# VectorE's transpose of a head's P, moved behind all 16 chunks of the next head's first K piece

## The chip, the cores and the metric

The kernel runs on one core of a Trainium2 chip. The metric is the device time of one execution in microseconds (us). Three runs of the kernel before took 666.61, 669.48 and 670.76 us; their median, 669.48, is the time that the changed kernel is compared with.

## What is computed

One decode step of a transformer block, one token, in bfloat16. Attention has 32 query heads in 8 groups of 4, each group with one K/V head ("head" below means one of these 8), and a cache of 65,536 positions. A gated layer follows. Cut to what matters:

```python
# D = 512, Hq = 32, Hkv = 8, Sk = 65536, Dh = 128, F = 1792
q = layernorm(x) @ wq                                  # 32 heads of 128
scores = einsum("bhqd,bhkd->bhqk", q, k) * Dh ** -0.5  # 4 queries share a K head
p = softmax(scores, axis=-1)
o = einsum("bhqk,bhkd->bhqd", p, v)
h = x + o.reshape(1, 1, 4096) @ wo
g, u = layernorm(h) @ w_gate, layernorm(h) @ w_up
return h + (sigmoid(g) * u) @ w_down
```

K and V of one head are 16 MiB each, 256 MiB for all; the weights are small beside them.

## The kernel before

**Loads.** K and V of a head are each loaded in two pieces of 8 MiB (`PIECES`), one `dma_start` a piece, all from SyncE's queue (line 330, called from lines 338 to 342). A piece is 16 chunks of 2,048 positions. For heads h from 1 on, the loop issues K{h}.0, V{h-1}.0, K{h}.1, V{h-1}.1, in this order, and each waits until its place in the `ring` buffer is free:

- K{h}.0 waits for the marker F{h-1}.1, V{h-1}.0 for the end of the PV products of the head before it, K{h}.1 for the marker F{h}.0, V{h-1}.1 for PV{h-1}.1, the end of the first half of the PV products.
- The two K pieces overlap in the ring (`AT`: they begin at chunk 0 and chunk 4), and `ORDER` has VectorE read chunks 4 to 15 of the first piece first. So the marker F{h}.0 stands behind the 12th chunk of the piece, and F{h}.1 behind the 12th chunk of the second. A marker is a memset of one element on VectorE (line 520).

Heads are one apart: while head h's K is read and scored, V of head h-1 is multiplied with P of head h-1.

**VectorE** transposes each K chunk (line 517, 128 x 1024 as 4-byte words, from `ring` into one of 8 slots of `ktw`). From the second block on, a transpose waits until TensorE has done with the slot 8 chunks before (`S{b-1}.{c}`). It also takes the maximum of the scores (line 524), a few steps of the softmax, the transpose of P (`transposed`, lines 570 to 575: four transposes of 128 x 512 out of `P_sb` into `PT_sb`) and the sum of the denominators with its reciprocal (lines 580 and 581).

**TensorE** scores a block of 8 chunks with 32 matmuls of 512 columns (`pe_scores`). A head has four blocks, r = 0 to 3; two blocks are one K piece. Behind block r = 1 of head h it takes the denominators' matmul of head h-1 (line 578, which waits for the last transpose of P) and the first half of PV of head h-1; behind block r = 3 the second half. **ScalarE** writes P (line 563: exp of the scores, four instructions a head) at the end of a head, ahead of the next head's first block.

**Order.** Instructions are recorded by Python loops and then put out. Heads 1 to 7 are one hardware loop on VectorE and on TensorE: what is recorded under a part's name (`P.part`) becomes one section of the loop body, and `dve_flow` writes the order of VectorE's sections out by hand. `A0` to `A3` are the blocks' chunk transposes (A3 with the maxima and the softmax steps), `A4` the four transposes of P, `B0` the denominators' sum. Each engine runs its own instructions in order; engines wait for each other by semaphores.

Numbering in the text: in loop round h, "first half" means the blocks r = 0 and 1 (piece K{h}.0), "second half" the blocks r = 2 and 3 (piece K{h}.1).

Of the kernel before, what the change touches and what calls it, by code (L numbers as in the profile page):

```python
# [35 lines left out]
class Prog:  # L36
# [14 lines left out]
    def op(self, eng, fn, deps=(), name=None, to=None, times=1):  # L51
        assert name is None or name not in self.where, name
        self.ops[eng].append(dict(fn=fn, deps=[d for d in deps if d], name=name, dma=None, to=to, times=times, part=self.part.get(eng)))
        if name:
            self.where[name] = (eng, len(self.ops[eng]) - 1)
# [160 lines left out]
def bass_sequential_preLN__gqa_block_cached__glu_gated_glu__decode_kernel(  # L216
# [22 lines left out]
    with ExitStack() as es:  # L239
# [72 lines left out]
        P = Prog(nc, es)  # L312
# [187 lines left out]
        def dve_block(b):  # L500
            h, r = b // NR, b % NR
            for c in range(NC):
                n, s = b * NC + c, r * NC + c
                j = ORDER[s]
                q = sum(j >= z for _, z in PIECES)
                at = (first_chunk("K", h, q) + j - PIECES[q][0]) * CH
                src = ring[:, at:at + CH].bitcast(fp32)
                dst = ktw[:, (n % NKT) * CH:(n % NKT + 1) * CH].bitcast(fp32)
                if h == 0:
                    deps = [f"K0.{q}{'ab'[j % 16 // 8]}"] if s in (0, 4, 16, 24) else []  # L510
                    if s == 0:
                        deps.append("q")
                else:
                    deps = [f"K{h}.{q}"] if s in (0, 16) else []
                if r:
                    deps.append(f"S{b - 1}.{c}")
                op("dve", lambda e, d=dst, sr=src: e.transpose(d, sr), deps, f"T{b}.{c}", to="T")  # L517
                mark = ({15: 0, 31: 1} if h == 0 else {11: 0, 27: 1}).get(s)
                if mark is not None:
                    op("dve", lambda e, m=4 * h + mark: e.memset(scr[:, m:m + 1], 0.0), (), f"F{h}.{mark}")  # L520
            if b % NR == NR - 1:
                for k in range(NR):
                    u = b - NR + 1 + k
                    op("dve", lambda e, u=u: e.tensor_reduce(M_sb[:, u % 4:u % 4 + 1], ps(u % NS, 0, 512), AX.X, ALU.max),  # L524
                       [f"S{b}.{NC - NR + k}"], f"mx{u}", to="D")
                op("dve", lambda e: e.memset(scr[:, 32 + b // NR:33 + b // NR], 0.0), (), f"G{b // NR}")

        def pe_scores(b):
            h, r = b // NR, b % NR
            for half in range(NC // NR):  # L530
                for je in range(4):
                    if half == je == 0:
                        P.part["pe"] = ("An" if r else "As", b)
                    elif half == 0 and je == 1:
                        P.part["pe"] = ("A", b)
                    for k in range(NR):
                        c = half * NR + k
                        deps = [f"T{b}.{c}"] if je == 0 else []
                        if r == 0 and half == je == k == 0:
                            deps.append(f"W{h}")  # L540
                        op("pe", lambda e, r=r, half=half, je=je, k=k, c=c: mm_at(
                            e, ps(k, 0, 512), at_reg(ktw, reg(e, half * 4 + je) if half or je else R["w"], [[KTW_ROW, 128], [1, 128]]), e.lower_ap(kt_ap(c, je)),
                            r == half == je == 0, 128, kept=k > 0),
                           deps, f"S{b}.{c}" if je == 3 else None, to="Q" if je == 3 else None)
# [25 lines left out]
        def transposed(h):  # L570

            for b in range(NR * h, NR * h + NR):
                op("dve", lambda e, b=b: e.transpose(PT_sb[:, (b % 4) * 512:(b % 4 + 1) * 512],  # L573
                                                     P_sb[:, (b % 4) * 512:(b % 4 + 1) * 512]),
                   [f"E{b}"], f"PT{b}", to="PT" if b % NR == NR - 1 else None)

        def denominators(h):
            op("pe", lambda e: e.matmul(ps(MISC, 132, 136), lhsT=lsel[:, :], rhs=L_sb[:, :], start=True, stop=True),  # L578
               [f"PT{NR * h + NR - 1}"], f"l{h}", to="Q")
            op("dve", lambda e: e.tensor_reduce(lsum[:, :], ps(MISC, 132, 136), AX.X, ALU.add), [f"l{h}"], f"ls{h}", to="D")  # L580
            op("dve", lambda e: e.reciprocal(rl[:, :], lsum[:, :]), [f"ls{h}"], f"rl{h}")
# [9 lines left out]
        def pv(h, r, rounds):  # L591
            P.part["pe"] = ("B", (h, r, rounds))
            name = f"PV{h}.{r}" + "a" * (rounds == 6)
            for k in range(2):
                for tq in range(4):
                    i = k * 8 + tq
                    op("pe", lambda e, tq=tq, i=i: mm_at(
                        e, ps(PO, 0, 512, 32 * tq, 32 * tq + 32),
                        at_reg(PT_sb, reg(e, i) if i else R["p"], [[PT_ROW, 128], [4, 32]]),
                        at_reg(ring, reg(e, i + 4) if i else R["v"], [[RING, 128], [1, 512]]), False, 32, 32 * tq),  # L600
                       (), name if k and tq == 3 else None, times=rounds)

        def head_out(h):
            op("act", lambda e: e.activation(po_sb[:, :], ps(PO, 0, 512), AF.Copy, scale=rl[:, :]),  # L604
               [f"PV{h}.{NR - 1}", f"rl{h}"], f"po{h}", to="po")
            for t in range(4):
                op("pe", lambda e, t=t: e.matmul(ps(OX, 0, 4), lhsT=po_sb[:, t * 128:(t + 1) * 128],  # L607
                                                 rhs=sel_bf[:, 8 * t:8 * t + 8:2], start=(t == 0), stop=(t == 3)),
                   [f"po{h}"] if t == 0 else (), f"ox{h}" if t == 3 else None)
            op("act", lambda e: e.activation(O2[:, GS * h:GS * h + GS], ps(OX, 0, 4), AF.Copy), [f"ox{h}"], f"o2.{h}")  # L610
            if h + 1 < HKV:
                clear_out(h + 1)
# [54 lines left out]
        def columns():  # L667

            for nt in range(4):
                lhsT = bass.AP(tensor=yr, offset=nt, ap=[[D, 1], [4, 128]])  # L670
                op("pe", lambda e, lhsT=lhsT, nt=nt: e.matmul(ps(YT, nt, nt + 1), lhsT=lhsT, rhs=one_f[0:1, 0:1], start=(nt == 0),  # L671
                                                              stop=False, skip_group_check=True), ["yrs"] if nt == 0 else ())
# [86 lines left out]

        def dve_flow(e, section):  # L760
            with e.Fori(1, HKV):
                for p in ("A0", "A4", "A1", "B0", "A2", "A3"):
                    section(p)

        P.flow = {"pe": pe_flow, "dve": dve_flow}
# [4 lines left out]
        for i in range(HKV + 1):  # L770
            loop, last = 0 < i < HKV, i == HKV
            for r in range(NR):
                P.part = {"dve": (f"A{r}", i) if loop else None}
                if not last:
                    dve_block(NR * i + r)
                    pe_scores(NR * i + r)
                P.part = {"dve": ("A4", i) if loop else None}
                if i and r == 0:
                    transposed(i - 1)
                if i and r == 1:  # L780
                    P.part = {"pe": ("V0", i), "dve": ("B0", i) if loop else None}
                    denominators(i - 1)
                    op("pe", lambda e: None, [f"V{i - 1}.0", f"z{i - 1}"])
                    pv(i - 1, r, 6)
                    pv(i - 1, r, 2)
                if i and r == 3:
                    if last:
                        P.part["pe"] = ("L", i)
                        project7()
                        columns()  # L790
                    P.part["pe"] = ("V3", i)
                    op("pe", lambda e: None, [f"V{i - 1}.1"])
                    pv(i - 1, r, 6)
                    if last:
                        P.part["pe"] = ("VL", i)
                        op("pe", lambda e: None, [f"V{i - 1}.1b"])
                    pv(i - 1, r, 2)
                    P.part["pe"] = ("O", i)
                    head_out(i - 1)
                if not last and r == 3:  # L800
                    P.part = {"pe": ("X", i), "dve": ("A3", i) if loop else None}
                    softmax(i)
# [78 lines left out]
```

## Time and profile before

| what | value |
|---|---|
| three runs, median | 666.61, 669.48, 670.76; 669.48 us |
| the profiled execution, its own time | 666.32 us |
| its span, from the first to the last instruction | 665.0 us |
| TensorE / VectorE / ScalarE busy | 60% / 53% / 6% of the span |
| time of queue 1's DMA packets, as a share of 16 engines' span | 98.9% |
| read from HBM | 282.33 MB |
| mean granted TensorE clock | 0.794 |

"Busy" counts compute instructions alone; waits, branches and the issue of DMAs are not in it. The chain of waits follows back from the last instruction what released each step; a DMA stands in it from its issue to its landing, so time that it spent queued behind another transfer is in it too. In the views below a row begins with its start and its duration in us, and "L517" is line 517 of the kernel.

### The profile page before, as it was taken

The numbers are of one execution on the slowest core, as the hardware profiler recorded it, in microseconds if no ns is written. First come the engines' busy times: TensorE is split into PE (matmuls) and PEld (weight loads), VectorE is DVE, ScalarE is ACT, GpSimd is POOL, SyncE is SP. The second block draws the span as 40 slices with busy tenths as digits, with TensorE's granted clock in tenths as the row PEclk, the third lists the DMA queues.
The fourth block names the chain that finished last, engine by engine and source line by source line (L and its number), as shares of the span: only waits on it lengthen the run. The fifth ranks groups of instructions, "written<-read, shape, count | busy, mean of one in ns | idle before, by whom it ended". The sixth has DMA issues, their size and how long they took to land.

```text
span 665.0 us, 6197 instructions
## 1 busy us (share of the span) xinstructions
PE 399.3 (60%) x2316; PEld 68.5 (10%) x1548; DVE 350.2 (53%) x427; ACT 42.9 (6%) x114; POOL 3.6 (1%) x17
## 2 busy tenths in 40 slices
PE   2788562927647273764829366482746738285485
PEld 1100010100101001010100101010010101001132
DVE  3498943819265380936628193562908457092102
ACT  1100200020000200002000200002000020002001
POOL 1000000000000000000000000000000000000000
PEclk9789795967859698785968779596886959778776
DMA  9999999999999999999999999999999999999996
GB/s 400 426 436 442 442 434 442 438 406 426 438 442 442 434 386 442 442 438 442 386 442 438 442 434 390 442 442 438 414 398 438 434 438 402 438 426 442 415 420 277
DMA packets 6370, 282.33 MB, mean 425 GB/s; under 512 B 737, under 2 KB 738, under 8 KB 1250
## 3 DMA queue, kind: packets, MB, share of 16 engines
q1 hardware_dynamic: 6338, 282.33, 98.9%
q10 hardware_dynamic: 32, 0.00, 0.0%
HBM read 282.33 MB, written 0.00 MB: 425 GB/s over the span
## 4 chain that ended last, share of the span: by engine, by line
DMA 59%; DVE 33%; PE 5%; issue 3%; ACT 0%; SPq 0%; PEldq 0%
DMA ring<-in_A_k_cache_dram 56%; DVE ktw L517 30%; DMA ring<-in_A_v_cache_dram 4%; PE PS L430 3%; DVE PT_sb L573 2%; PE PS L822 0%; PE PS L671 0%; PE PS L840 0%; DVE hh L832 0%; PE PS L626 0%; PE PS L636 0%; ACT po_sb L604 0%; DVE yr L665 0%; DVE hhT L835 0%; PE PS L391 0%
## 5 line engine op out<-in xcount | busy, mean ns | idle before, releaser
L430 PE MATMUL PS<-ktw 128*128 128x512 bf16 x1024 | 280.8, 420 | 178.4 <-DVE ktw L517 170.8
L517 DVE STREAM_TRANSPOSE ktw<-ring 128x1024 f32<-128x1024 f32 x256 | 291.6, 1207 | 158.4 <-DMA ring<-in_A_k_cache_dram 158.4
L430 PE MATMUL PS<-ring,PT_sb 128*32 x1024 | 80.9, 409 | 45.8 <-issue 41.9
L430 PEld LDWEIGHTS PS<-ktw 128*128 x256 | 26.2, 102 | 421.0 <-issue 252.9
L604 ACT ACTIVATE po_sb<-PS,rl 128x512 bf16<-128x512 f32 x8 | 5.5, 687 | 533.6 <-PE PS L430 533.6
L430 PEld LDWEIGHTS PS<-ring,PT_sb 128*32 x1024 | 21.2, 116 | 104.2 <-issue 101.4
L552 DVE TENSOR_REDUCE gmj<-PS 1x4 f32<-1x128 f32 x8 | 2.2, 279 | 53.1 <-PE PS L550 53.1
L524 DVE TENSOR_REDUCE M_sb<-PS 128x1 f32<-128x512 f32 x32 | 19.9, 684 | 19.3 <-PE PS L430 19.3
L563 ACT ACTIVATE P_sb<-PS,negmax 128x512 bf16<-128x512 f32 x32 | 21.6, 685 | 0.3
L573 DVE STREAM_TRANSPOSE PT_sb<-P_sb 128x512 bf16<-128x512 bf16 x32 | 19.9, 675 | 1.7 <-ACT P_sb L563 1.7
L580 DVE TENSOR_REDUCE lsum<-PS 128x1 f32<-128x4 f32 x8 | 1.3, 163 | 23.0 <-PE PS L578 23.0
L430 PE MATMUL PS<-ktw,xz 128*8 x32 | 8.4, 429 | 3.6 <-DMA ktw<-in_A_wq_dram 3.6
L620 DVE TENSOR_TENSOR Lw<-O,blk_of 128x896 bf16<-128x896 bf16 (+1 forms) x2 | 1.4, 683 | 12.8 <-ACT O L610 12.8
L430 PE MATMUL PS<-ktw,O 128*1 x26 | 7.9, 474 | 0.0
L629 DVE CAST O<-PS 128x28 bf16<-128x28 f32 (+1 forms) x2 | 0.3, 175 | 14.2 <-PE PS L626 14.2
L550 PE MATMUL PS<-identf,gm 128*1 128x128 f32 x16 | 4.3, 364 | 5.7 <-issue 3.6
L557 PE MATMUL PS<-one_f,gmrep 1*128 1x1 f32 x16 | 4.2, 332 | 5.0 <-DVE gmrep L554 5.0
L475 DVE STREAM_TRANSPOSE qt<-qh 32x512 bf16<-32x512 bf16 x1 | 0.7, 699 | 11.1 <-ACT qh L472 11.1
L563 ACT ACTIVATION_READ_ACCUMULATOR P_sb<-PS,negmax 128x1 f32 x32 | 6.5, 202 | 0.0
L607 PE MATMUL PS<-sel_bf,po_sb 128*128 128x4 bf16 x32 | 2.1, 171 | 6.3 <-ACT po_sb L604 6.3
L665 DVE COPY yr<-PS 1x512 f32<-1x512 f32 x1 | 0.7, 678 | 8.6 <-PE PS L663 8.6
L490 ACT ACTIVATE PS<-zcol 128x512 f32<-128x512 bf16 x8 | 5.0, 621 | 0.0
(88 smaller groups left out, 68.0 us busy)
## 6 DMA issues: line engine op xcount, KB each, us to landing
ring<-in_A_k_cache_dram SPq DMA_DIRECT2D x4, 4096.0 KB, 35.0
ring<-in_A_v_cache_dram SPq DMA_DIRECT2D x1, 6144.0 KB, 33.5
ktw<-in_A_wq_dram SPq DMA_DIRECT2D x1, 4096.0 KB, 12.2
ktw<-in_A_wo_dram SPq DMA_DIRECT2D x1, 3584.0 KB, 18.6
ring<-in_A_v_cache_dram SPq DMA_DIRECT2D x1, 2048.0 KB, 37.9
ring<-in_B_w_gate_dram SPq DMA_DIRECT2D x1, 1792.0 KB, 23.8
ring<-in_B_w_up_dram SPq DMA_DIRECT2D x1, 1344.0 KB, 26.7
ring<-in_B_w_down_dram SPq DMA_DIRECT2D x1, 1024.0 KB, 29.3
```

The costliest lines, as they stand in the source:

```text
L430: return e.add_instruction(mybir.InstMatmult(name=nc.get_next_instruction_name(), engine=mybir.EngineType.PE, ins=[rhs, lhsT], outs=[e.low ...
L490: op("act", lambda e: e.activation(ps(PO, 0, 512), bass.AP(tensor=zcol, offset=0, ap=[[1, 128], [0, 512]]), AF.Copy), ["zcol"] if h == 0 e ...
L517: op("dve", lambda e, d=dst, sr=src: e.transpose(d, sr), deps, f"T{b}.{c}", to="T")
L524: op("dve", lambda e, u=u: e.tensor_reduce(M_sb[:, u % 4:u % 4 + 1], ps(u % NS, 0, 512), AX.X, ALU.max), [f"S{b}.{NC - NR + k}"], f"mx{u}" ...
L550: op("pe", lambda e: e.matmul(ps(MISC, 0, 128, 0, 1), lhsT=gm[:, :], rhs=identf[:, :], start=True, stop=True), [f"gm{h}"], f"gmT{h}", to="Q")
L552: op("dve", lambda e: e.tensor_reduce(gmj[:, :], ps(MISC, 0, 128, 0, 1).rearrange("p (i a c) -> p a i c", a=4, c=NC), AX.XY, ALU.max), [f" ...
L557: op("pe", lambda e: e.matmul(ps(MISC, 128, 129), lhsT=gmrep[0:1, :], rhs=one_f[0:1, 0:1], start=True, stop=True), [f"gmrep{h}"], f"neg{h}")
L563: op("act", lambda e, b=b: e.activation(P_sb[:, (b % 4) * 512:(b % 4 + 1) * 512], ps(b % NS, 0, 512), AF.Exp, bias=negmax[:, k:k + 1], sca ...
L573: op("dve", lambda e, b=b: e.transpose(PT_sb[:, (b % 4) * 512:(b % 4 + 1) * 512], P_sb[:, (b % 4) * 512:(b % 4 + 1) * 512]), [f"E{b}"], f" ...
L604: op("act", lambda e: e.activation(po_sb[:, :], ps(PO, 0, 512), AF.Copy, scale=rl[:, :]), [f"PV{h}.{NR - 1}", f"rl{h}"], f"po{h}", to="po")
L607: op("pe", lambda e, t=t: e.matmul(ps(OX, 0, 4), lhsT=po_sb[:, t * 128:(t + 1) * 128], rhs=sel_bf[:, 8 * t:8 * t + 8:2], start=(t == 0), s ...
L620: op("dve", lambda e: e.tensor_tensor(Lw[i][:, :].rearrange("p (j c) -> p j c", j=n), bass.AP(tensor=O2, offset=j0, ap=[[NQ, 128], [1, n], ...
```

## The change

`transposed(i - 1)`, the four transposes of P of head i-1, is recorded behind block r = 1 of head i instead of behind block r = 0, and VectorE's loop body takes its section `A4` behind `A1` instead of ahead of it. So VectorE runs all 16 chunks of the first K piece with the marker F{i}.0 behind the 12th, then the four transposes of P, then the denominators' sum. The instructions and their number are the same, and so are TensorE's, ScalarE's and SyncE's programs. The second half of a head, head 0 (outside the loop) and all that follows the scores of head 7 keep their order.

```diff
         def dve_flow(e, section):
             with e.Fori(1, HKV):
-                for p in ("A0", "A4", "A1", "B0", "A2", "A3"):
+                for p in ("A0", "A1", "A4", "B0", "A2", "A3"):
                     section(p)
...
                 if not last:
                     dve_block(NR * i + r)
                     pe_scores(NR * i + r)
-                P.part = {"dve": ("A4", i) if loop else None}
-                if i and r == 0:
+                if i and r == 1:
+                    P.part = {"dve": ("A4", i) if loop else None}
                     transposed(i - 1)
-                if i and r == 1:
                     P.part = {"pe": ("V0", i), "dve": ("B0", i) if loop else None}
                     denominators(i - 1)
                     op("pe", lambda e: None, [f"V{i - 1}.0", f"z{i - 1}"])
```

## The prediction

> **What bounds the kernel now.** I read the page first, for the engines, the DMA and the chain; then the chain of waits in order of time over one round of the loop; then the windows between the landings of K pieces over the whole loop.
>
> ```profile
> PE 399.3 (60%) x2316; PEld 68.5 (10%) x1548; DVE 350.2 (53%) x427; ACT 42.9 (6%) x114; POOL 3.6 (1%) x17
> ...
> DMA packets 6370, 282.33 MB, mean 425 GB/s; under 512 B 737, under 2 KB 738, under 8 KB 1250
> ...
> DMA 59%; DVE 33%; PE 5%; issue 3%; ACT 0%; SPq 0%; PEldq 0%
> ```
>
> No compute engine is near full, and the chain is DMA (59%) and VectorE (33%) in turn. Two readings fit that: the loads run back to back and VectorE's share only hangs in their shadow, or VectorE issues loads late and the queue runs dry. The chain over round 2 of the loop, landing of K2.0 to landing of K3.0, shows the steps:
>
> ```profile
> 123.91 24.93 DMA ring<-in_A_k_cache_dram
> 148.84 0.02 issue
> 148.86 0.05 DVE ktw L517
> 148.92 1.11 issue
> 150.03 7.96 DVE ktw L517 x7
> 158.00 2.37 DVE PT_sb L573 x4
> 160.37 4.54 DVE ktw L517 x5
> 164.91 0.02 issue
> 164.92 23.50 DMA ring<-in_A_k_cache_dram
> 188.42 0.02 issue
> 188.45 13.67 DVE ktw L517 x13
> 202.12 0.02 issue
> 202.14 24.93 DMA ring<-in_A_k_cache_dram
> ```
>
> K2.0 lands at 148.84. VectorE does 8 chunks, the four transposes of P (2.37 us), 4 more chunks, and the marker lets K2.1 go at 164.92, 16.08 us after the landing. K2.1 lands at 188.42; in this half 12 chunks go through without a break, and K3.0 goes at 202.14, 13.72 us after the landing. From here I call the time from a K.0 landing to the K.1 landing a first half, and from there to the next K.0 landing a second half. Each brings two pieces, V of the head before and the next K piece, 16.78 MB in all. The windows between the landings, first and second halves in turn, over the loop (columns: stretch, its length, busy time of PE, PEld, DVE, ACT and POOL with counts, granted clock, DMA share, GB/s):
>
> ```profile
> 70.29:110.19 39.90, 21.89 (x130) 3.30 (x82) 20.88 (x23) 2.97 (x9) 0.00 (x0) 0.80 0.98 420
> 110.19:148.84 38.65, 23.47 (x136) 3.75 (x88) 21.32 (x25) 4.68 (x13) 0.00 (x0) 0.76 1.00 434
> 148.84:188.42 39.58, 23.56 (x130) 3.38 (x82) 20.88 (x23) 0.00 (x0) 0.00 (x0) 0.76 0.99 427
> 188.42:227.06 38.64, 23.02 (x136) 3.56 (x88) 21.32 (x25) 4.68 (x13) 0.00 (x0) 0.81 1.00 434
> 227.06:267.20 40.14, 22.07 (x130) 3.28 (x82) 20.88 (x23) 0.00 (x0) 0.00 (x0) 0.84 1.02 436
> 267.20:305.85 38.65, 23.44 (x136) 3.75 (x88) 21.32 (x25) 4.68 (x13) 0.00 (x0) 0.76 1.00 434
> 305.85:344.52 38.67, 23.57 (x130) 3.39 (x82) 20.88 (x23) 0.00 (x0) 0.00 (x0) 0.76 0.97 412
> 344.52:383.21 38.69, 23.82 (x136) 3.78 (x88) 21.44 (x25) 4.68 (x13) 0.00 (x0) 0.76 1.00 434
> 383.21:422.56 39.35, 22.50 (x130) 3.29 (x82) 20.88 (x23) 0.00 (x0) 0.00 (x0) 0.80 1.00 426
> 422.56:461.30 38.74, 23.79 (x136) 3.76 (x88) 21.44 (x25) 4.68 (x13) 0.00 (x0) 0.76 1.00 433
> 461.30:502.00 40.70, 22.59 (x130) 3.36 (x82) 20.88 (x23) 0.00 (x0) 0.00 (x0) 0.79 1.00 422
> 502.00:540.67 38.67, 23.67 (x136) 3.80 (x88) 21.32 (x25) 4.68 (x13) 0.00 (x0) 0.76 1.00 434
> 540.67:580.43 39.76, 22.34 (x130) 3.29 (x82) 20.88 (x23) 0.00 (x0) 0.00 (x0) 0.80 0.97 412
> ```
>
> The six second halves take 38.64 to 38.74, 232.04 in all, mean 38.67: 16.78 MB in 38.67 us is 434 GB/s, and six that agree to 0.1 us with a DMA share of 1.00 are loads back to back. The seven first halves carry the same bytes and take 38.67 to 40.70, 278.10 in all, mean 39.73. (A window's GB/s counts packets by their start, so a single row of it can run a few per cent high or low; the lengths carry the argument.) So the bound is the stream of loads, and it loses 1.06 us a round somewhere in the first half. The second half has no such loss.
>
> What differs is how early the next piece is asked for. A half of 38.67 us is two equal pieces of 19.33. V1.0 therefore ends near 148.84 + 19.33 = 168.17, and K2.1, issued at 164.92, came 3.25 us ahead of that. V1.1 ends near 188.42 + 19.33 = 207.75, and K3.0, issued at 202.14, came 5.61 us ahead. A lead of 5.6 us costs nothing six times out of six; a lead of 3.25 us costs between 0 and 2.03 (40.70 - 38.67), six times out of seven more than 0.6. I read it as the lead being a little short: some of the 16 DMA engines run dry before their share of the next piece is ready.
>
> **The change, step by step.** Removed from the first half's path to the marker: the four transposes of P, 2.37 us. The marker then follows 12 unbroken chunks, which the second half shows at 13.67, so K{h}.1 goes 13.7 us after the landing in place of 16.08, and its lead grows from 3.25 to 19.33 + 0.02 - 13.72 = 5.6 us, the second half's lead. The first half then should take the second half's time: 7 x 38.67 = 270.7 in place of 278.1, which is **7.4 us less**. Bounds: 0 if the lead is not what costs; 7.6 if every first half came down to the 38.64 of the best second half (278.10 - 270.48). I take 7.4, because the second half is the nearest row: same chunks, same lead, same kind of piece.
>
> The gain is in the stream of loads itself. Behind the last first half (580.43) nothing is edited, and each load and product that follows hangs on that landing, directly or through the queue, so the end moves with it. TensorE's clock can rise at another point of the tail; I allow 1 us either way.
>
> Added: the four transposes now stand behind the 16th chunk, ahead of the denominators' sum (B0), with the next round's A2 chunks queued behind both. On VectorE no time is added (the count is the same, and A2 waits for K{h}.1 anyway). Who waits for them is TensorE, with the denominators' matmul, and behind it the first half of PV, and behind that V{h-1}.1 on SyncE's queue:
>
> ```profile
> 169.48 2.97 PE L430 MATMUL PS<-ktw 128*128 128x512 bf16 x13 [0.75 <-DVE ktw L517]
> 172.29 0.28 PE L578 MATMUL PS<-L_sb,lsel 128*128 128x4 f32 x2
> ```
>
> ```profile
> 203.18 3.45 DVE L517 STREAM_TRANSPOSE ktw<-ring 128x1024 f32<-128x1024 f32 x3
> ```
>
> ```profile
> 206.69 2.98 PE L430 MATMUL PS<-ktw 128*128 128x512 bf16 x13 [0.75 <-DVE ktw L517]
> ```
>
> ```profile
> 180.23 0.33 SPq L330 DMA_DIRECT2D ring<-in_A_v_cache_dram  x1
> ```
>
> In the second half the 16th chunk ends at 206.63, 18.2 us after the landing, and TensorE's scores at 209.67, 21.25 after. With P behind the chunks, P ends 18.2 + 2.4 = 20.6 after the landing, 0.65 us before TensorE gets there: hidden. The scores of the first half now end 23.6 us after the landing (172.45 - 148.84); without the break they end at 21.25, so PV starts 2.4 us earlier and V{h-1}.1 goes about 29.0 us after the landing in place of 31.4 (180.23 - 148.84). It is needed 5.6 us before K{h}.1 ends, at 38.67 - 5.6 = 33.0. So the cover has 4 us to spare. If the 0.65 us is gone, the price is still nothing until the four transposes come 4 us late. K{h+1}.0 hangs on the second half alone; V{h-1}.0 is needed by PV at 21.3 and lands at 19.33.
>
> The break had one use: TensorE is slow at the start of a half, and the break let it catch up.
>
> ```profile
> 153.54:158.98 5.44, 5.44 (x13) 0.54 (x4) 5.44 (x6) 0.00 (x0) 0.00 (x0) 0.50 0.89 386
> ```
>
> At a granted clock of 0.50, 13 matmuls take 5.44 us, 0.42 each. Chunk transposes 9 to 12 reuse the slots of chunks 1 to 4, which TensorE frees with its 13th to 16th matmul. Even at 0.42 throughout, that is about 4.7 + 12 x 0.42 = 9.7 us after the landing, and the 12th transpose starts at 13.67 x 11 / 12 = 12.5. So the marker is not delayed. Chunks 13 to 16 may wait a little; the second halves, with the same clock at their start and no break, show what: VectorE 21.32 in four of six and 21.44 in two, 0.12 us.
>
> The sum: 665.0 - 7.4 = 657.6 for the span, and 666.32 - 7.4 = 658.9 for that execution's own time. It was faster than all three runs; from their median the same 7.4 gives 662.1. First halves differ by up to 2.03 us within one execution, so part of the runs' 4.15 us of spread may well be this same loss and go with it. I put the median in between, at **660.5 us**.
>
> A rule of the Trainium skill speaks against the gain. DMA: Bandwidth & Descriptors, section Specifications, gives about 0.6 us to the first byte for a load issued as these are; by it a lead of 3.25 us would already be enough, and the sum would be 0. The rows disagree: 39.73 on average with that lead and 38.67 with 5.6.
>
> **The rivals.** *The first half's loss is not the lead's.* K{h}.1 might be slow in itself, by its place in the ring or in HBM, or because VectorE and TensorE work beside its start. Then its earlier issue only queues longer, and the time stays 669.5. For it: the loss scatters from 0 to 2.03 us at an unchanging lead, and one first half (305.85) lost nothing. Against: six second halves without any loss, with the same engines at work at the same point. The Trainium skill's 0.6 us, above, would make this the likely case; the rows do not bear it out. Chance 0.14.
>
> *Half of it.* Some of the loss is the lead's and some the piece's: 3.7 us, 665.8. Chance 0.08.
>
> *Slower: TensorE's half clock takes the place of the break.* If, without the pause, the clock stayed at 0.50 for the whole first half, the 60 matmuls behind the first four would take 60 x 0.42 = 25.2 us and the scores end at 29.9 after the landing; PV takes 7.8 more (172.45 to 180.23), and V{h-1}.1 goes at 37.7, about 1 us ahead of K{h}.1's end. A lead of 3.25 costs 1.06; one of 1 costs up to 2.25 more, 3.3 a round against 1.06 now, so up to 7 x 2.25 = 16 us: 669.5 + 16 = 685. It decides from the point at which V{h-1}.1 goes later than 35.4 us after the landing (a lead of 3.25). Against: without the break TensorE waits less, and the second halves run unbroken at a mean clock of 0.76 to 0.81. Chance 0.08.
>
> **How the numbers follow.** The forecast has the remaining 0.70. About 1% is what a measurement of this kernel can tell from no change; 1% below the median is 662.8. Forecast: 656.5 to 664, most of it (0.60) below 662.8, 0.10 above. With half of it (0.08) and no effect (0.14), within 1% has 0.32; slower has 0.08. The range, 656.5 to 668, holds the forecast, half the gain and the lower part of no effect; it leaves out the slower case and the rest of no effect, about 0.2.
>
> **What would show it.** In the chain, K{h}.1 issued 13.7 us after K{h}.0's landing, and no transpose of P in the chain. In the windows, first halves at 38.7 like the second, with 434 GB/s. On TensorE, the denominators' matmul released by the scores rather than by P, about 21.3 us after the landing; V{h-1}.1 issued near 29. Wrong if the issue moves by 2.4 us and the first halves stay at 39.7 (the lead was not the cause), or if second halves lengthen (the load of V{h-1}.1 came late), or if gaps open between chunks 9 and 16.

## The result, and the profile after

The changed kernel takes 658.39 us (median of 6 runs, 657.74 to 659.2); the kernel before, run beside it and counted with its earlier runs, 668.26 us (6 runs, 664.77 to 670.76). The ratio is 0.9853, with a 95% interval of 0.982 to 0.9887. The forecast was 660.5 us with a range of 656.5 to 668. The profiled execution took 658.92 us against 666.32 before, and its span went from 665.0 to 657.6 us, which is the 7.4 us of the sum. One run of the kernel before, beside the first four experiments below, took 1201.72 us and is in none of the ratios.

From the page of the changed kernel:

```profile
PE 403.7 (61%) x2316; PEld 68.8 (10%) x1548; DVE 350.7 (53%) x427; ACT 42.9 (7%) x114; POOL 3.6 (1%) x17
...
DMA packets 6370, 282.33 MB, mean 429 GB/s; under 512 B 737, under 2 KB 738, under 8 KB 1250
...
q1 hardware_dynamic: 6338, 282.33, 99.3%
```

The engines run the same instructions and are busy for about as long (TensorE 4.4 us longer, at a mean granted clock of 0.780 in place of 0.794); the bytes come faster, 429 in place of 425 GB/s. The windows between the landings of K pieces, the first four and the last of the loop (columns as before):

```profile
70.63:109.22 38.59, 21.83 (x130) 3.22 (x82) 20.89 (x23) 2.97 (x9) 0.00 (x0) 0.82 1.00 435
109.22:147.92 38.70, 24.75 (x136) 3.84 (x88) 21.44 (x25) 4.68 (x13) 0.00 (x0) 0.72 1.00 434
147.92:186.50 38.58, 22.72 (x130) 3.28 (x82) 20.89 (x23) 0.00 (x0) 0.00 (x0) 0.81 1.00 435
186.50:225.18 38.68, 23.52 (x136) 3.74 (x88) 21.32 (x25) 4.68 (x13) 0.00 (x0) 0.76 1.00 434
...
534.28:572.88 38.60, 23.20 (x130) 3.22 (x82) 20.88 (x23) 0.00 (x0) 0.00 (x0) 0.77 1.00 435
```

Before, a first half took anything from 38.67 to 40.70; now all seven take 38.58 to 38.60, and the six second halves 38.68 to 38.70. Where the 7.4 us came from: first halves 278.10 to 270.11 (-7.99), second halves 232.04 to 232.14 (+0.10), the landing of K1.0 70.29 to 70.63 (+0.34), and what follows the landing of K7.1 84.57 to 84.72 (+0.15). SyncE's queue in round 2 of the loop (the issue of K2.1, of V1.1 and of K3.0):

```profile
161.63 0.33 SPq L330 DMA_DIRECT2D ring<-in_A_k_cache_dram  x1
178.05 0.33 SPq L330 DMA_DIRECT2D ring<-in_A_v_cache_dram  x1
200.21 0.33 SPq L330 DMA_DIRECT2D ring<-in_A_k_cache_dram  x1
```

K2.1 goes 161.63 - 147.92 = 13.71 us after the landing of K2.0, in place of 16.08, and K3.0 13.71 after that of K2.1 at 186.50, as before. VectorE in the same round, in order of time:

```profile
147.94 14.81 DVE L517 STREAM_TRANSPOSE ktw<-ring 128x1024 f32<-128x1024 f32 x13 [6.85 <-DMA ring<-in_A_k_cache_dram]
161.52 0.06 DVE L520 MEMSET scr<- 1x1 f32 x1
162.68 3.45 DVE L517 STREAM_TRANSPOSE ktw<-ring 128x1024 f32<-128x1024 f32 x3
166.05 2.45 DVE L573 STREAM_TRANSPOSE PT_sb<-P_sb 128x512 bf16<-128x512 bf16 x4
169.31 0.16 DVE L580 TENSOR_REDUCE lsum<-PS 128x1 f32<-128x4 f32 x1 [0.81 <-PE PS L578]
```

The chunks run without a gap, the marker (L520) stands behind the 12th, P behind the 16th. The chain of waits is of no more use here: it goes back from the end to 635.83 and stops. That by itself does not show that only the stream of loads is left: the chains of the experiments `gap4` and `gap12` below stop in the same way (at 644.45 and 664.25), and these kernels lose 1.1 and 4.1 us a round.

### The profile page after: what moved, and what is told of

Same layout as the page of the kernel before. It is cut to its first block, busy times and chain, and to the rows that moved or that the text cites. A ratio compares the mean times of both kernels' runs of the same rounds, so it can differ in the third digit from the quotient of the medians.

```text
span 657.6 us, 6197 instructions
## 1 busy us (share of the span) xinstructions
PE 403.7 (61%) x2316; PEld 68.8 (10%) x1548; DVE 350.7 (53%) x427; ACT 42.9 (7%) x114; POOL 3.6 (1%) x17
## 5 line engine op out<-in xcount | busy, mean ns | idle before, releaser
L430 PE MATMUL PS<-ktw 128*128 128x512 bf16 x1024 | 277.8, 421 | 161.3 <-DVE ktw L517 157.5
L430 PE MATMUL PS<-ring,PT_sb 128*32 x1024 | 87.0, 430 | 51.4 <-issue 47.3
L559 ACT ACTIVATE negmax<-PS 128x1 f32<-128x1 f32 x8 | 1.4, 172 | 55.1 <-PE PS L557 55.1
```

Of the source, the lines that this page charges most:

```text
L430: return e.add_instruction(mybir.InstMatmult(name=nc.get_next_instruction_name(), engine=mybir.EngineType.PE, ins=[rhs, lhsT], outs=[e.low ...
L559: op("act", lambda e: e.activation(negmax[:, k:k + 1], ps(MISC, 128, 129), AF.Copy, scale=-att_scale), [f"neg{h}"], f"negmax{h}")
```

## The experiments

Theory: what cost time was the short **lead**, the time from the issue of a load to the end of the load ahead of it in the queue. Rivals: the place of P itself (a break inside the piece, TensorE getting P sooner or later), or a K{h}.1 that is slow in itself. "Spare" transposes below write what the transposes of P write into tiles that nothing reads; they only take VectorE's time. In the edits, `...` stands for lines left out.

**The late marker without the old place of P** (`gap4`):

```diff
-                for p in ("A0", "A1", "A4", "B0", "A2", "A3"):
+                for p in ("A0", "S", "A1", "A4", "B0", "A2", "A3"):   # S: four spare transposes
...
```

> The changed kernel, with the four transposes of P once more into spare tiles at their old place, between the 8th and the 9th chunk. The lead theory (what costs is that K{h}.1 is asked for only 3.25 us before V{h-1}.0 has ended): the marker is late again, K{h}.1 goes 16.1 us after the landing, first halves are 39 to 40.7 us again, the time 664 to 671 as before the change. The rival that the place of P itself matters (TensorE has P later or sooner, the order on VectorE): P stands where the change put it, so 658 to 660.

666.97 us, ratio to the kernel before 0.9999 (0.9981 to 1.0017). The whole gain is gone, although P stands where the change put it. Its first three windows:

```profile
70.41:110.27 39.86, 23.27 (x130) 3.31 (x82) 23.25 (x27) 2.96 (x9) 0.00 (x0) 0.80 0.98 421
110.27:148.95 38.68, 23.57 (x136) 3.75 (x88) 21.32 (x25) 4.68 (x13) 0.00 (x0) 0.76 1.00 434
148.95:188.97 40.02, 23.59 (x130) 3.31 (x82) 23.26 (x27) 0.00 (x0) 0.00 (x0) 0.80 1.02 436
```

First halves are back at 39.9 and 40.0, and at 39.66 on average over the loop. Of the six second halves four stay at 38.7, and two later ones take 39.1 and 39.2. K2.1 was issued at 165.03, again 16.08 us after the landing.

**The break without the late marker** (`mark`):

```diff
-                for p in ("A0", "A1", "A4", "B0", "A2", "A3"):
+                for p in ("A0", "A1", "A4", "A1b", "B0", "A2", "A3"):   # A1 ends with the marker, A1b: chunks 13 to 16
...
```

> The changed kernel, with the four transposes of P right behind the marker, so between the 12th and the 13th chunk: the piece is broken again, the marker is not delayed. The lead theory: K{h}.1 goes 13.7 us after the landing, first halves of 38.7 us, 657 to 660. The rival that the break inside the piece costs time on VectorE or TensorE: 664 to 671.

658.72 us, ratio 0.9874 (0.9825 to 0.9923). VectorE and TensorE in round 2:

```profile
147.66 13.63 DVE L517 STREAM_TRANSPOSE ktw<-ring 128x1024 f32<-128x1024 f32 x12 [7.26 <-DMA ring<-in_A_k_cache_dram]
161.22 0.70 DVE L577 STREAM_TRANSPOSE PT_sb<-P_sb 128x512 bf16<-128x512 bf16 x1
161.23 0.06 DVE L520 MEMSET scr<- 1x1 f32 x1
161.85 1.85 DVE L577 STREAM_TRANSPOSE PT_sb<-P_sb 128x512 bf16<-128x512 bf16 x3
163.63 4.58 DVE L517 STREAM_TRANSPOSE ktw<-ring 128x1024 f32<-128x1024 f32 x4
```

```profile
168.26 2.98 PE L430 MATMUL PS<-ktw 128*128 128x512 bf16 x13 [0.75 <-DVE ktw L517]
171.08 0.28 PE L582 MATMUL PS<-L_sb,lsel 128*128 128x4 f32 x2
171.29 1.66 PE L430 MATMUL PS<-ring,PT_sb 128*32 x24
```

The piece is broken, the scores end at 171.24, 23.6 us after the landing as in the kernel before, and still nothing is lost. What the change did to TensorE is worth nothing either way.

**An early request without touching VectorE** (`split`), on the kernel before. The last 4 chunks of K{h}.1 have a place in the ring that K{h}.0 does not use, so their load waits only for `G{h-1}`, VectorE's marker at the end of the head before (line 526):

```diff
-            load("K", h, 1, [f"F{h}.0"], "kb", f"K{h}.1")
+            load("K", h, 1, [f"G{h - 1}"], "kc", f"K{h}.1b", (28, 32))
+            load("K", h, 1, [f"F{h}.0"], "kb", f"K{h}.1", (16, 28))
...
```

> The kernel before, VectorE's order untouched, but K{h}.1 in two loads: its last 4 chunks (2 MiB, a place in the ring that K{h}.0 does not use) are asked for right behind V{h-1}.0, the other 12 behind the marker as before. The lead theory: the marker still comes 16.1 us after the landing, but 2 MiB (4.8 us of stream) are queued by then, so the lead is about 8 us and first halves are 38.7: 657 to 660. The rivals that K{h}.1 is slow in itself, or that the break costs by itself: 664 to 671.

658.71 us, ratio 0.9874 (0.9826 to 0.9923). VectorE in round 2, P between the chunks as ever (line numbers are one higher):

```profile
147.68 9.13 DVE L518 STREAM_TRANSPOSE ktw<-ring 128x1024 f32<-128x1024 f32 x8 [7.21 <-DMA ring<-in_A_k_cache_dram]
156.73 2.45 DVE L574 STREAM_TRANSPOSE PT_sb<-P_sb 128x512 bf16<-128x512 bf16 x4
159.10 5.75 DVE L518 STREAM_TRANSPOSE ktw<-ring 128x1024 f32<-128x1024 f32 x5
163.63 0.06 DVE L521 MEMSET scr<- 1x1 f32 x1
```

The windows of rounds 1 and 2, first halves:

```profile
70.34:108.98 38.64, 23.22 (x130) 3.35 (x82) 20.88 (x23) 3.16 (x9) 0.00 (x0) 0.77 1.00 434
147.66:186.42 38.76, 23.75 (x130) 3.40 (x82) 20.88 (x23) 0.00 (x0) 0.00 (x0) 0.76 1.01 433
```

The marker is as late as it was (163.63, 16 us after the landing), and the gain is all there: the seven first halves take 38.69 on average. So the lead does it, not where P stands.

**The loss moved to the other half** (`second4`), on the changed kernel:

```diff
-                for p in ("A0", "A1", "A4", "B0", "A2", "A3"):
+                for p in ("A0", "A1", "A4", "B0", "A2", "S", "A3"):   # S: four spare transposes
...
```

> The changed kernel, with four spare transposes of P between the 8th and the 9th chunk of the second half, where before and after the change have none. The lead theory: K{h+1}.0 (and V7.0 in the last round) goes 16.1 us after the landing of K{h}.1, a lead of 3.25 us, and now the second halves lose 0 to 2 us each, 6 to 10 in all: 664 to 670, with first halves at 38.6. The rival that K{h}.1 is slow in itself: 658 to 660, no loss in the second halves.

666.29 us, ratio to the kernel before 0.9978 (0.9955 to 1.0001). Its first four windows:

```profile
70.46:109.06 38.60, 22.71 (x130) 3.26 (x82) 21.00 (x23) 3.16 (x9) 0.00 (x0) 0.77 1.00 435
109.06:148.91 39.85, 23.86 (x136) 3.77 (x88) 23.69 (x29) 4.68 (x13) 0.00 (x0) 0.80 0.98 421
148.91:187.54 38.63, 23.11 (x130) 3.26 (x82) 21.00 (x23) 0.00 (x0) 0.00 (x0) 0.77 1.00 434
187.54:227.34 39.80, 23.86 (x136) 3.76 (x88) 23.69 (x29) 4.68 (x13) 0.00 (x0) 0.80 1.01 433
```

Now the second halves lose 1.1 to 1.2 us in these rows, 1.0 on average over the loop (39.69 against 38.69), and the first ones 0.16 (38.75 against 38.59). K{h}.1 is not slow in itself.

**How much lead is needed** (`gap2`, `gap3`, `gap6`, `gap8`, `gap12`): more or fewer spare transposes before the marker. The first two are the changed kernel with two and three of them in section S; the others are the kernel before, P at its old place, with two, four and eight:

```diff
-                for p in ("A0", "A4", "A1", "B0", "A2", "A3"):
+                for p in ("A0", "S", "A4", "A1", "B0", "A2", "A3"):   # S: two (gap6) or four (gap8); gap12: four behind chunk 1, four behind chunk 12
...
```

> The changed kernel with two spare transposes of P between the 8th and the 9th chunk: lead 5.6 - 1.2 = 4.4 us. If a load needs a fixed time L from its issue until all DMA engines can go on with it, the loss of a round is L less the lead; a lead of 3.25 lost about 1.06 (profile) to 1.4 us (median), so L is 4.3 to 4.65 and the loss here 0 to 0.25 a round: 658 to 660.5. The rival that any delay of the marker costs alike: half of the way, 662 to 664.

> The changed kernel with three spare transposes: lead 5.6 - 1.8 = 3.8 us. Fixed L of 4.3 to 4.65: a loss of 0.5 to 0.85 a round, 662 to 664.5. The rival that any delay costs alike: three quarters of the way, 664.5 to 666.5.

> The kernel before with four spare transposes beside those of P, all between the 8th and the 9th chunk: lead 3.25 - 2.37 = 0.9 us. Fixed L: 2.37 us more loss in each of the seven rounds, 668 + 16.6 = 682 to 686. A loss that does not grow with the delay (the slow start of a load, whatever its lead): 666 to 670.

> The kernel before with two spare transposes of P beside those of P, all between the 8th and the 9th chunk: lead about 2.05 us, between the kernel before (3.25, median 667.5) and the kernel with four spares (0.9, 670.6). If the loss saturates, as that one suggests (1.7 us a round at a lead of 0.9), 667.5 to 670.6. If its 670.6 was a chance of that one kernel and each us of lead less costs one us more, 675 to 678.

> The kernel before with eight spare transposes, four behind the first chunk and four behind the 12th: the marker comes 20.8 us after the landing, 1.5 us after V{h-1}.0 has ended. With 0.9 us of lead a round lost about 1.7, so a load on idle engines would be ready 0.9 + 1.7 = 2.6 us or a little less after its issue. With the queue empty nothing can hide it: a loss of 1.5 + 2.1 to 2.6 a round, 683 to 688. If the loss stays at 1.7 whatever the lead, 670 to 672.

The lead is 19.33 us less the time from the landing to the issue of K{h}.1; the loss is the mean of the seven first halves, from the windows between the landings of each kernel, less the 38.59 of the changed kernel:

| kernel | lead, us | first halves, mean | loss a round | median (runs) |
|---|---|---|---|---|
| changed | 5.6 | 38.59 | 0 | 658.39 (657.74 to 659.2) |
| gap2 | 4.4 | 38.61 | 0.02 | 658.88 (658.45 to 659.41) |
| gap3 | 3.8 | 38.82 | 0.23 | 661.04 (659.75 to 664.9) |
| gap4 | 3.25 | 39.66 | 1.07 | 666.97 (666.18 to 668.32) |
| before | 3.25 | 39.73 | 1.14 | 668.26 (664.77 to 670.76) |
| gap6 | 2.05 | 40.15 | 1.56 | 669.49 (666.61 to 673.59) |
| gap8 | 0.9 | 40.26 | 1.67 | 670.57 (669.83 to 671.26) |
| gap12 | -1.5 | 42.64 | 4.05 | 687.54 (686.64 to 687.96) |

One first half of each of gap2, gap8 and gap12:

```profile
147.63:186.24 38.61, 22.93 (x130) 3.28 (x82) 22.07 (x25) 0.00 (x0) 0.00 (x0) 0.81 1.00 435
```

```profile
149.45:189.61 40.16, 26.11 (x130) 3.44 (x82) 23.25 (x27) 0.00 (x0) 0.00 (x0) 0.71 0.98 418
```

```profile
151.68:194.25 42.57, 23.53 (x130) 3.29 (x82) 25.62 (x31) 0.00 (x0) 0.00 (x0) 0.78 0.93 394
```

Second halves take 38.67 to 38.74 on average in these kernels, 38.86 in gap4, so the load of V{h-1}.1, which the spares delay as well, is not what they lose.

gap8 and gap3 came out below what was expected of a fixed time L, from a load's issue until the engines can go on with it, taken from the lead of 3.25 (682 to 686 and 662 to 664.5): that model was wrong. A load issued on idle engines (gap12) loses the 1.5 us of the empty queue and 2.55 more; a lead of 0.9 then should lose 2.55 - 0.9 = 1.65, and lost 1.67. From there to a lead of 4 the loss stays well above that line: at 3.25 the line would give nothing, and 1.1 is lost. gap6, in between, scatters most, by 7.0 us.

**A small load first** (`two`), on the kernel before: K{h}.1 in two loads, both behind the late marker.

```diff
-            load("K", h, 1, [f"F{h}.0"], "kb", f"K{h}.1")
+            load("K", h, 1, [f"F{h}.0"], "kb", f"K{h}.1", (16, 20))
+            load("K", h, 1, (), "kc", f"K{h}.1b", (20, 32))
...
```

> The kernel before with K{h}.1 in two loads, both behind the late marker, first 4 chunks (2 MiB), then 12. If the time from issue to readiness is the same for every load, the first small load is as late as the whole one was: 664 to 671. If it grows with the size of the load, the first one is ready in about a quarter of the time and its 4.8 us of stream cover the second: 657 to 661.

665.28 us, ratio 0.9973 (0.9957 to 0.9989). Some 2 of the 9 to 10 us come back; most of the loss does not shrink with the size of the first load.

## Why the prediction was right, and where it was off

**The bound and its loss.** Right, and shown from both sides: with the lead short again the gain goes (gap4), and with the lead long by another way it comes without the change (split). Of the rivals, a K{h}.1 that is slow in itself falls with split and second4, and half the gain with the windows. The prediction counted for the first rival that one first half (305.85) lost nothing at the same lead. It did lose: a window ends with the last of the 16 DMA engines, and in that round the last one kept its time while the others fell behind. The mean over the 16 engines, from landing to landing, is 39.87 us there and at least 38.97 in each first half of the kernel before, against 38.62 to 38.64 in the changed kernel.

**The step of the marker.** 13.7 us after the landing and a lead of 5.6 were forecast; 13.71 to 13.84 was measured, in both halves. No stall worth more than that opened up to the marker: in the three first halves with 13.84 VectorE's busy time is 21.00, in the others 20.88 or 20.89, against 20.88 before. The 0.12 us is what the prediction read from the second halves.

**The size.** For the profiled execution the sum held to 0.1 us: 657.6 for the span, 658.92 for its own time against 658.9. The medians are 9.9 us apart in place of 7.4. The term that was mis-sized is the loss of a round: 1.06 us in the one profiled execution, which lies 2 us below the median, and 9.9 / 7 = 1.4 us by the medians. The kernel before has medians of 667.5 to 667.9 in the three batches of 13 to 19 runs beside the experiments; by these it is 1.3 to 1.4. That the spread of the runs would go with the loss was written as likely and came true: 6.0 us between the kernel's runs before, 1.5 after. So the point was put too high by weighing 662.1, worked out from the median before, against 658.9; the execution's own sum alone was the better forecast.

**P's new cover.** P was to end 20.6 us after the landing and the scores at 21.25; they end at 20.6 (166.05 + 2.45 - 147.92) and 21.2. But V{h-1}.1 was to go at 29.0 and goes at 30.1 (178.05 - 147.92), up to 30.8 in other rounds. The step that failed is that PV would take the same time from an earlier start: from the end of the scores to the issue it takes 8.9 us (169.16 to 178.05) in place of 7.8. TensorE in the kernel before, and in the changed kernel, behind the denominators' matmul:

```profile
172.29 0.28 PE L578 MATMUL PS<-L_sb,lsel 128*128 128x4 f32 x2
...
172.50 1.60 PE L430 MATMUL PS<-ring,PT_sb 128*32 x24
```

```profile
169.00 0.28 PE L578 MATMUL PS<-L_sb,lsel 128*128 128x4 f32 x2
169.66 0.63 PE L430 MATMUL PS<-ring,PT_sb 128*32 x8 [0.38 <-issue]
170.63 0.63 PE L430 MATMUL PS<-ring,PT_sb 128*32 x8 [0.34 <-issue]
```

Before, 24 matmuls of PV came in one burst; now each group of 8 comes alone, with a wait for issue ahead of it. In the kernel `mark`, where P ends before the 13th chunk, the burst of 24 is back. It looks as if TensorE's instruction stream, which now reaches the wait for P before P is done (168.50), can no longer run ahead; that it does so is argued from these rows, not tried by itself. It costs nothing, because V{h-1}.1 is needed only at 33.0: `mark` issues it 31.3 to 33.4 after the landing, 5.2 us or more ahead of the end of K{h}.1, and takes the same time.

**The slower rival.** TensorE's half clock was no trouble: mean granted clocks of first halves are 0.77 to 0.82, against 0.76 to 0.84 before. The price of this rival was too high as well: it put a lead of 1 at up to 3.3 us a round, and a lead of 0.9 lost 1.67 (gap8).

## What to carry to other kernels

Where a queue of loads is the bound, look at when each load is asked for against the end of the load ahead of it, and compare a place in the loop that loses nothing with one that does: the two halves of this loop gave the price before anything was built. What delays the release of a buffer is then on the path, however little of the span it fills; move it behind the release, or ask early for the part of the load whose place is free. About 4.4 us of lead were enough here, and more bought next to nothing.

## What the runs showed of the hardware

A load of 8 MiB that was issued when the queue had run dry cost 2.55 us of the stream beyond the dry time (gap12). Its first 16 packets began 0.95 to 1.96 us after the start of the issue and took 2.4 to 3.6 us; in the stream a packet of 64 KiB takes 2.42. To cost nothing such a load had to be issued about 4.4 us ahead of the end of the load before it, not 2.55: leads of 3.8, 3.25 and 2.05 us lost 0.2, 1.1 and 1.6 us.

In between, the 16 DMA engines no longer finish together. The trace records when each of them has done its share of a piece: the first and the last are 1.3 to 2.8 us apart at the landings of K{h}.1 in the kernel before, and 0.8 in the changed kernel. So the engine that is done first had less lead than the 3.25 us of the last: 0.6 to 2.7 us. Around the start of K{h}.1 in the kernel before, 92 packets of 64 KiB took more than 2.6 us, up to 3.9, and 85 of them began 0.95 to 4.5 us after the issue of K{h}.1; in the changed kernel, where the first engine is done 4.6 us or more after that issue, none took more than 2.48. It looks as if a load is served slowly in the first 4 us or so behind its issue, and an engine that reaches it within that time pays. The trace does not say to which load a packet belongs, and what makes these packets slow stays open.

The Trainium skill (DMA: Bandwidth & Descriptors, Specifications) gives about 0.6 us to the first byte of such a load. On the dry queue the trace agrees: the first packet began 0.62 us after the end of the issue, which takes 0.33. By that figure alone a lead of 2.05 would have cost nothing; the runs disagree, with 1.6 us lost.
